# Two attention mixes on one core: the last four tiles of projected rows move from the projection stage into the attention steps

## The chip, the cores and the metric

The kernel runs on one core of a Trainium2 chip. The core has a matrix engine (TensorE, PE in the profile, with its weight loads shown apart as PEld), a vector engine (VectorE, DVE), a scalar engine for activations and copies (ScalarE, ACT), a general engine (GpSimd, POOL) and a queue engine (SyncE, SP) that issues most DMAs. Each engine works through its own instructions in order, and waits on semaphores for the others. The metric is the device time of one execution in microseconds, as the median of several runs.

## The reference

Two attention layers read the same input and are mixed by a gate. Layer A is a full multi-head attention with 32 heads of 18 columns; layer B has 32 query heads but one shared key and value.

```python
def _A_ref(x, wqkv, wo):
    B, S, D = x.shape                       # 1, 2048, 576
    H = 32; Dh = D // H                     # 18
    qkv = (x @ wqkv).reshape(B, S, 3, H, Dh).transpose(2, 0, 3, 1, 4)
    q, k, v = qkv[0], qkv[1], qkv[2]
    scores = jnp.einsum("bhqd,bhkd->bhqk", q, k) * Dh ** -0.5
    p = softmax(scores, axis=-1)
    o = jnp.einsum("bhqk,bhkd->bhqd", p, v)
    return o.transpose(0, 2, 1, 3).reshape(B, S, D) @ wo

def _B_ref(x, wq, wk, wv, wo):
    q = (x @ wq).reshape(B, S, H, Dh).transpose(0, 2, 1, 3)
    k = x @ wk                              # one key and one value for all heads
    v = x @ wv
    scores = jnp.einsum("bhqd,bkd->bhqk", q, k) * (Dh ** -0.5)
    p = softmax(scores, axis=-1)
    o = jnp.einsum("bhqk,bkd->bhqd", p, v)
    return o.transpose(0, 2, 1, 3).reshape(B, S, H * Dh) @ wo

g = sigmoid((x * gate_w).sum(-1, keepdims=True))
return g * a + (1 - g) * b
```

## The kernel before

**Numbers in two parts.** Matmuls run on rounded operands (type float32r). To keep accuracy, an operand is split into a rounded high part ("h") and the rounded remainder ("l"), and a product is taken as hh + lh + hl. `split` makes the parts: a copy that rounds, then a subtraction that rounds. `PROJ` lists the 14 matmuls of one projection (5 chunks of the 576 input columns, the last one holding high and low part in its two halves).

**Heads.** There are 64 heads (`NU`): the 32 of layer B first, then the 32 of layer A. The query and key rows of all heads, with the gate and the shared key and value, are the 1792 output rows of one wide projection. They are cut into 14 tiles (`MT`) of 128 rows by 2048 positions, and a tile into four banks of 512 positions, the size of one PSUM bank.

**Stage one, projection.** The transposed input X stays in SBUF in two parts. `project` forms one bank: 14 matmuls of 512 columns (L156), then `leave` rounds the high part out of PSUM on ScalarE (L162), takes the low part on VectorE (L168), and stores both to the DRAM tensor `qk_d` (POOL's DMA queue). For tiles that hold keys, the difference of the first two key banks goes to `kd_d`. Tiles 0 to 2 are formed while X arrives; tiles 3 to 9 follow as 28 banks in a row. Between banks, SP loads the rows of the first heads back (`bring_row`, one load after each bank and a second after each fourth). In the same stretch the value weights of layer A are loaded, rounded (`split_w`, ScalarE and VectorE) and stored to `wv_d`. The last four tiles, 10 to 13, are formed in 16 further banks, each mixed with six maxima of the first heads; there `leave_lead` evicts on ScalarE and subtracts on Pool, and `store_x` writes X to the DRAM tensor `x_d`. After that X's place in SBUF is given to other tiles.

**Stage two, steps.** 1024 steps follow: head u has steps 16u to 16u+15, one for each block of 128 keys. A step has four scores matmuls (`step_scores`, L530) into a ring of three PSUM banks (`ps`), each read by an exponential on ScalarE (L538); four matmuls for the row maxima of a head 22 steps ahead (`step_max`, L478) into a ring of four banks (`pm`), read by VectorE's maximum (L487); and 16 short matmuls that sum the weighted values (`step_pv`, L544). Scores and maxima use different rows of the array and run in pairs. One pair of key banks in a while is taken together ("x" and "y" in the patterns): ScalarE takes the relu of a difference (L481), and VectorE adds and takes the maximum in one instruction (L484).

**What sets the order.** Each engine's order is written by hand. `emit` walks through a pattern string: "s" a scores matmul with its exponential, "m" a maximum, "x" and "y" the paired one, a digit so many quarters of the sums' matmuls, "U" one unit of other work from the list `todo`. `PLAIN` covers two steps without a unit, `SPARSE` eight steps with one, `DENSE` two steps with one. `SPARSE` is used for 256 steps from step 10 (`VB`), for the value units, and again for 256 steps from step 522, for the first output units; steps 266 to 521 and 778 to 945 are plain. `when(T, f)` calls f at step T. `slow` holds generators with small pieces (normalisation, output weights), of which one piece is issued every other step, mostly on Pool and SP. At steps 10, 26, 42 and so on, `max_rows` turns a head's maxima into two more rows of its queries: VectorE, Pool, then two DMA steps on SP.

**Units.** A value unit (`value_units`) multiplies a block of X, read back from `x_d`, by one half of layer A's value weights, read back from `wv_d`: 14 matmuls of 288 columns (L442) into one `pm` bank, one ScalarE eviction (L444), one store. An output unit (`out_proj`) has 12 matmuls of 288 columns (L692) and one eviction (L695) into the accumulator `oacc`, which takes over the value units' place in SBUF at step 274 (`open_oacc`).

## Time and profile before

| | us |
|---|---|
| median of 3 runs | 2738.43 (2738.14 to 2738.99) |
| the profiled execution's own time | 2739.16 |
| its span | 2737.4 |
| TensorE busy | 2729.2 |
| ScalarE busy | 2443.6 |
| VectorE busy | 2391.7 |
| Pool busy | 271.4 |

How to read it. A group's row gives line, engine, operation, what it writes and reads with shapes, count, busy time and the mean duration of one in ns, and behind a second bar the engine's idle time before such instructions, with what ended it. A row of the timeline gives start, duration, engine, line, operation and count; idle time stands in square brackets. Instructions of one engine overlap: the next one starts before the last one has ended, so the distance of two starts, not the duration, is what an instruction costs its engine. A row of the windows gives the stretch, its length, the busy time of the engines shown with the number of instructions, the granted clock, the DMA engines' busy share and GB/s; with a line given, it counts that line's instructions alone. SPq is the issue of a DMA on the SP queue, not its duration. TensorE is shown as busy nearly all the time because a matmul that waits inside the pipeline counts as busy; whether it waited is seen from the distances of the starts.

### The profile page before, as it was taken

Reading aid. Unit: us, or ns where it says so; the run is one execution under the profiler, and the core shown is the slowest. Engines: PE = TensorE matmul, PEld = TensorE weight load, DVE = VectorE, ACT = ScalarE, POOL = GpSimd, SP = SyncE. Lnnn points to the kernel's source line nnn. Section 1 sums busy time; section 2 is a strip of 40 time slices with the busy share of each in tenths; the row PEclk is TensorE's granted clock in tenths of the full one; section 3 lists DMA queues with packets and bytes.
Section 4 is the critical chain, followed back from the end, with each engine's and each line's share of the span. In section 5 each row is a group of like instructions: output and inputs, shape, how many; then the busy total and the mean of one; then the engine's idle time right before and its main releaser. Section 6 shows DMA issues by size and latency. Waiting matters only on the chain.

```text
span 2737.4 us, 60422 instructions
## 1 busy us (share of the span) xinstructions
PE 2729.2 (100%) x23542; PEld 1301.5 (48%) x23542; DVE 2391.7 (87%) x4495; ACT 2443.6 (89%) x4787; POOL 271.4 (10%) x407
## 2 busy tenths in 40 slices
PE   9999999999999999999999999999999999999999
PEld 8874444454454333333334444444444333334555
DVE  4488888888889999999999898888989999998883
ACT  4338999999999999999999999999999999998776
POOL 2371000010001000100110001000100011011002
PEclk9999999999999999999999999999999999999999
DMA  8883211122111101211133213222321223224312
GB/s 285 326 303 125 60 55 38 59 80 75 42 57 57 56 27 34 65 48 31 47 95 108 87 58 95 93 70 75 100 87 46 68 86 99 67 79 120 101 46 89
DMA packets 145954, 242.09 MB, mean 88 GB/s; under 512 B 53650, under 2 KB 99810, under 8 KB 134092
## 3 DMA queue, kind: packets, MB, share of 16 engines
q1 hardware_dynamic: 131268, 187.13, 22.7%
q0 software_dynamic: 13504, 49.88, 4.8%
q8 instruction: 185, 3.03, 0.5%
q10 hardware_dynamic: 896, 1.23, 0.1%
q14 instruction: 101, 0.83, 0.1%
HBM read 149.61 MB, written 79.78 MB: 84 GB/s over the span
## 4 chain that ended last, share of the span: by engine, by line
PE 99%; DMA 0%; DVE 0%; ACT 0%; issue 0%; ACTq 0%
PE acc L544 38%; PE ps L530 32%; PE pm L478 14%; PE ps L156 6%; PE pm L692 4%; PE pm L442 2%; PE acc L555 1%; PE pm L530 0%; DMA xsh<-xT 0%; PE ps L478 0%; PE ps L692 0%; DVE mx L487 0%; DMA wst<-wall 0%; ACT pt L538 0%; DVE oacc L701 0%; PE pm L739 0%
## 5 line engine op out<-in xcount | busy, mean ns | idle before, releaser
L538 ACT ACTIVATE pt<-ps 128x512 f32<-128x512 f32 x4048 | 2133.8, 612 | 119.9 <-PE pm L478 55.3
L487 DVE TENSOR_REDUCE mx<-pm 128x1 f32<-128x512 f32 x3068 | 1942.5, 684 | 193.9 <-PE pm L478 145.7
L530 PE MATMUL ps<-qs,ksb 56*128 56x512 f32 x2688 | 899.2, 436 | 0.1
L478 PE MATMUL pm<-ksb,qs 54*128 54x512 f32 x2336 | 794.7, 437 | 0.1
L530 PEld LDWEIGHTS ps<-qs,ksb 56*128 56x128 f32 x2688 | 435.0, 184 | 493.8 <-ACT pt L538 465.0
L544 PE MATMUL acc<-pt,vb 128*19 128x256 f32 (+3 forms) x6656 | 579.3, 434 | 0.1
L544 PE MATMUL acc<-pt,vg 128*19 128x256 f32 (+3 forms) x6224 | 553.8, 443 | 0.0
L530 PE MATMUL ps<-qs,ksa 56*128 56x512 f32 x1360 | 454.6, 436 | 0.1
L478 PEld LDWEIGHTS pm<-ksb,qs 54*128 54x128 f32 x2336 | 370.9, 184 | 125.5 <-DVE mx L487 57.6
L478 PE MATMUL pm<-ksa,qs 54*128 54x512 f32 x1232 | 425.9, 439 | 0.0
L484 DVE CUSTOM_DVE_ANT_0 junk<-pm,xb 128x512 bf16<-128x512 f32 x500 | 340.3, 681 | 0.2
L530 PEld LDWEIGHTS ps<-qs,ksa 56*128 56x128 f32 x1360 | 219.4, 184 | 239.4 <-ACT pt L538 221.9
L481 ACT ACTIVATE xb<-pm 128x512 f32<-128x512 f32 x500 | 307.5, 615 | 0.0
L544 PEld LDWEIGHTS acc<-pt,vb 128*19 128x19 f32 x6656 | 125.6, 97 | 216.1 <-issue 192.7
L478 PEld LDWEIGHTS pm<-ksa,qs 54*128 54x128 f32 x1232 | 198.0, 184 | 56.5 <-DVE mx L487 26.0
L544 PEld LDWEIGHTS acc<-pt,vg 128*19 128x19 f32 x6224 | 118.8, 97 | 207.1 <-issue 183.2
L118 POOL CAST mh<-mt 128x32 fp32r<-128x32 f32 x64 | 13.4, 210 | 1719.7 <-DVE mt L495 1719.7
L478 PE MATMUL pm<-kdb,qs 54*128 54x512 f32 x372 | 153.3, 412 | 0.0
L162 ACT ACTIVATE phl<-ps 128x512 fp32r<-128x512 f32 x40 | 23.9, 598 | 71.4 <-PE ps L156 56.8
L156 PE MATMUL ps<-xh,wh 128*128 128x512 f32 (+1 forms) x300 | 85.6, 384 | 0.0
L156 PE MATMUL ps<-xh,wl 128*128 128x512 f32 (+1 forms) x300 | 83.3, 376 | 0.0
L168 DVE TENSOR_TENSOR phl<-ps,phl 128x512 fp32r<-128x512 f32 x40 | 27.7, 692 | 62.7 <-ACT phl L162 46.8
(144 smaller groups left out, 1471.9 us busy)
## 6 DMA issues: line engine op xcount, KB each, us to landing
qs<-qk SPq DMA_DIRECT2D x384, 144.0 KB
qk<-phl POOLq DMA_DIRECT2D x56, 512.0 KB, 5.6
ksa<-qk SPq DMA_DIRECT2D x132, 144.0 KB
ksb<-qk SPq DMA_DIRECT2D x66, 144.0 KB
xv<-x_d SPq DMA_DIRECT2D x16, 576.0 KB
onh<-oh SPq DMA_DIRECT2D x32, 256.0 KB
onl<-ol SPq DMA_DIRECT2D x32, 256.0 KB
oih<-onh SPq DMA_DIRECT2D x16, 512.0 KB
```

The source lines that it names most:

```text
L156: nc.tensor.matmul(fp[:, p0:p0 + g], w[a][:kr, k, :], X[b][:kr, k, x0 + p0:x0 + p0 + g], start=(n == 0), stop=(n == len(PROJ) - 1))
L168: nc.vector.tensor_tensor(hl[:, 1, :], fp, hl[:, 0, :].bitcast(F32), op=OP.subtract)
L442: nc.tensor.matmul(fp[:, 0:288], x[:kr, k if b == "h" else NKT + k, :], w[hf][a][:kr, k, :], start=(n == 0), stop=(n == len(PROJ) - 1))
L478: nc.tensor.matmul(pm, qs[u % 3][b:b + 54, i * P:(i + 1) * P], k, start=True, stop=True)
L481: nc.scalar.activation(MX["x", u, i], pm, AF.Relu)
L484: nc.vector.tensor_tensor_reduce(junk, pm, MX.pop(("x", u, i)), 1.0, -3e38, op0=OP.add, op1=OP.max, accum_out=MX[u][:, i, c:c + 1])
L487: nc.vector.tensor_reduce(MX[u][:, i, c:c + 1], pm, axis=AX.X, op=OP.max)
L530: nc.tensor.matmul(ps, kst(u)[b:b + 56, i * P:(i + 1) * P], qs[u % 3][b:b + 56, c * 512:(c + 1) * 512], start=True, stop=True)
L538: nc.scalar.activation(pt, ps, AF.Exp, scale=SCALE)
L544: nc.tensor.matmul(acc[32 * j:32 * j + 19, a:b], v_of(u, i), PT[u, i, j][:, a:b], start=(i == 0), stop=(i == 15), skip_group_check=True)
L555: nc.tensor.matmul(acc[32 * j:32 * j + 19, 256 * half + a:256 * half + b], v_of(NU - 1, i), pt[:, x + a:x + b], start=(i == 0), stop=(i == ...
L692: nc.tensor.matmul(fp[:, 0:288], x, y, start=(n == 0), stop=(n == len(ops) - 1))
```

## The change

Only tiles 0 to 9 are formed in stage one (`NT = 10`): tiles 3 to 5 as 12 banks in a row, tiles 6 to 9 in the 16 banks that are mixed with maxima. Three row loads follow each of the 12 banks. Tiles 10 to 13, which hold rows of heads 50 to 63, become 32 units of stage two (`row_units`), for which steps 274 to 529 now use `SPARSE`: half a bank each, 14 matmuls of 256 columns with X read back from `x_d` as the moving operand. A row unit evicts on ScalarE, rounds on ScalarE, subtracts on Pool, and stores by SP. Every eighth unit is followed by the next tile's weight split on Pool. The first output units start at step 530 instead of 522, and the accumulator is placed at step 530. The value weights no longer go through `wv_d`: the value units' prologue, at step 2, loads them in four pieces through two staging buffers and splits them on Pool.

```diff
-    wv_d = dram.tile([2, 2, P, NKT * 288], F32, name="wv_d")
...
-    LEAD_T = MT - 4
+    NT = 10
     def tiles_left(WN):
-        for mt in range(3, MT):
+        for mt in range(3, NT):
...
-    for n in range(4 * (LEAD_T - 3)):
-        mt, c, w = next(left)
-        if n in (0, 10):
-            vs = load_wv(n // 10)
-        project(mt, c, w)
-        bring_row()
-        if c == 3:
+    for n in range(4 * (NT - 4 - 3)):
+        project(*next(left))
+        for _ in range(3):
             bring_row()
-        if n in (8, 18):
-            store_wv(n // 10, vs)
...
+    def row_units():
+        pool = L["px"]
+        XR, WR = [], []
...
+        def load_xr(c):
+            XR.append(pool.tile([P, 2 * NKT - 1, 256], F32R, name="xr", bufs=2))
+            dma(XR[-1], x_d[:, :, 256 * c:256 * c + 256])
+        def next_w(mt):
+            W = {y: pool.tile([P, NKT, P], F32R, name=f"wr{y}") for y in "hl"}
+            split(WR.pop(0), W["h"], W["l"], nc.gpsimd, nc.gpsimd)
+            if mt + 1 < MT:
+                load_wr(mt + 1)
+            return W
...
+        for mt in range(NT, MT):
+            for c in range(8):
+                x = XR.pop(0)
+                if (mt, c) != (MT - 1, 7):
+                    load_xr((c + 1) % 8)
+                fp = ps_m.tile([P, 512], F32, name="pm")
+                for n, (a, b, k, kr) in enumerate(PROJ):
+                    nc.tensor.matmul(fp[:, 0:256], w[a][:kr, k, :], x[:kr, k if b == "h" else NKT + k, :],
+                                     start=(n == 0), stop=(n == len(PROJ) - 1))
+                hl = pool.tile([P, 2, 256], F32R, name="rhl", bufs=1)
+                st = pool.tile([P, 256], F32, name="rst", bufs=3)
+                nc.scalar.activation(st, fp[:, 0:256], AF.Copy)
+                nc.scalar.activation(hl[:, 0, :], st, AF.Copy)
+                nc.gpsimd.tensor_tensor(hl[:, 1, :], st, hl[:, 0, :].bitcast(F32), op=OP.subtract)
+                rs = slice(mt * P, (mt + 1) * P)
+                dma(qk_d[:, rs, 256 * c:256 * c + 256].rearrange("a p f -> p a f"), hl)
...
+                if c == 7 and mt + 1 < MT:
+                    w = next_w(mt + 1)
+                yield
...
         for hf in range(2):
-            for i, y in enumerate("hl"):
-                dma(w[hf][y], wv_d[hf, i].rearrange("p (k f) -> p k f", k=NKT))
+            src = wv[:, 288 * hf:288 * hf + 288]
+            main = src[0:512, :].rearrange("(p k) m -> p k m", p=P)
+            for k0, k1 in ((0, 3), (3, 5)):
+                t = L["pool"].tile([P, 16, 76], F32, name="vg", bufs=2)
+                t = t.rearrange("p a b -> p (a b)")[:, 0:288 * (k1 - k0)].rearrange("p (k f) -> p k f", f=288)
+                dma(t[:, 0:min(k1, 4) - k0, :], main[:, k0:min(k1, 4), :])
...
+                split(t, w[hf]["h"][:, k0:k1], w[hf]["l"][:, k0:k1], nc.gpsimd, nc.gpsimd)
...
-    when(VB + 8 * 32 + 8, open_oacc)
-    SEG = ((0, [P] * 4, 450, 518), (4, [P] * 4, 862, 942))
+    RB = VB + 8 * 33
+    when(RB - 8, lambda: (early("px"), todo.append(row_units()), pull(1)))
+    when(RB + 8 * 32, open_oacc)
+    SEG = ((0, [P] * 4, 450, 526), (4, [P] * 4, 862, 942))
...
-        elif any(b <= T < b + 8 * 32 for b in (VB, SEG[0][3] + 4)):
+        elif any(b <= T < b + 8 * 32 for b in (VB, RB, SEG[0][3] + 4)):
             emit(SPARSE, 1)
```

More of the change, by code (lines that the diff above doesn't have):

```diff
@@ L306, in gated_mix_kernel @@
                         WN = prep_w(W.pop(0))
-    vws = ExitStack()
-    vwp = vws.enter_context(tc.tile_pool(name="vwp", bufs=1, side="right"))
-    def load_wv(hf):
-        t = vwp.tile([P, NKT, 288], F32, name="vwst")
-        load5(t, wv[:, 288 * hf:288 * hf + 288])
-        return t
-    def store_wv(hf, st):
-        w = {y: vwp.tile([P, NKT, 288], F32R, name=f"vw{y}") for y in "hl"}
-        split_w(st, w, nc.vector)
-        for i, y in enumerate("hl"):
-            dma(wv_d[hf, i], w[y].rearrange("p k f -> p (k f)"), nc.gpsimd)
     def store_x(i):
@@ L332, in gated_mix_kernel @@
         load_q(u, put=later)
-    LEAD_T = MT - 4
+    NT = 10
     def tiles_left(WN):
-        for mt in range(3, MT):
+        for mt in range(3, NT):
             w = WN
-            if mt + 1 < MT:
+            if mt + 1 < NT:
                 WN = prep_w(W.pop(0))
-            if mt + 3 < MT:
+            if mt + 3 < NT:
                 W.append(load_w(mt + 3))
@@ L346, in gated_mix_kernel @@
     left = tiles_left(WN)
-    for n in range(4 * (LEAD_T - 3)):
-        mt, c, w = next(left)
-        if n in (0, 10):
-            vs = load_wv(n // 10)
-        project(mt, c, w)
-        bring_row()
-        if c == 3:
+    for n in range(4 * (NT - 4 - 3)):
+        project(*next(left))
+        for _ in range(3):
             bring_row()
-        if n in (8, 18):
-            store_wv(n // 10, vs)
     assert not rows_back
-    vws.close()
     small = ctx.enter_context(tc.tile_pool(name="small", bufs=1, side="left"))
@@ L404, in open_ph2 @@
         L["kds"] = [p2.tile([P, 512], F32R, name="kda"), kdb]
-        L["early"] = ExitStack()
-        L["vx"] = L["early"].enter_context(tc.tile_pool(name="vx", bufs=1, side="right"))
+        early("vx")
         for t in L["ks"][:2]:
@@ L410, in open_ph2, with early @@
                 dma(t[b + 54:b + 56, :], ones_r)
+    def early(name):
+        if "early" in L:
+            L["early"].close()
+        L["early"] = ExitStack()
+        L["px"] = L["early"].enter_context(tc.tile_pool(name=name, bufs=1, side="right"))
     def open_oacc():
@@ L415, in open_oacc, with load_wr @@
             .tile([P, 16, D], F32, name="oacc")
+    def row_units():
+        pool = L["px"]
+        XR, WR = [], []
+        def load_wr(mt):
+            WR.append(pool.tile([P, NKT, P], F32, name="wrst"))
+            load5(WR[-1], wall[mt])
+        def load_xr(c):
[7 more added lines that the diff above has]
+            return W
+        load_wr(NT)
+        load_xr(0)
+        w = next_w(NT)
+        yield
[15 more added lines that the diff above has]
+                dma(qk_d[:, rs, 256 * c:256 * c + 256].rearrange("a p f -> p a f"), hl)
+                if c < 2:
+                    KD[mt, c] = st
+                elif c < 4:
+                    cs = slice(256 * (c - 2), 256 * (c - 1))
+                    d = pool.tile([P, 256], F32, name="rd", bufs=1)
+                    nc.gpsimd.tensor_tensor(d, st, KD.pop((mt, c - 2)), op=OP.subtract)
+                    dhl = pool.tile([P, 2, 256], F32R, name="rdhl", bufs=1)
+                    split(d, dhl[:, 0, :], dhl[:, 1, :], nc.gpsimd, nc.gpsimd)
+                    dma(kd_d[rs, 0:2, cs], dhl)
+                    dma(kd_d[rs, 2, cs], dhl[:, 0, :])
+                if c == 7 and mt + 1 < MT:
+                    w = next_w(mt + 1)
+                yield
@@ L417, in value_units @@
     def value_units():
-        pool = L["vx"]
+        pool = L["px"]
         XV = {}
@@ L428, in value_units @@
         for hf in range(2):
-            for i, y in enumerate("hl"):
-                dma(w[hf][y], wv_d[hf, i].rearrange("p (k f) -> p k f", k=NKT))
+            src = wv[:, 288 * hf:288 * hf + 288]
[4 more added lines that the diff above has]
+                dma(t[:, 0:min(k1, 4) - k0, :], main[:, k0:min(k1, 4), :])
+                if k1 == NKT:
+                    for b in (0, 64):
+                        dma(t[b:b + 64, k1 - k0 - 1, :], src[512:576, :])
+                split(t, w[hf]["h"][:, k0:k1], w[hf]["l"][:, k0:k1], nc.gpsimd, nc.gpsimd)
         vst = [pool.tile([P, 16, 19], F32, name=f"vst{i}") for i in range(2)]
@@ L663, in out_proj @@
         nt = len(rows)
-        oacc = L["oacc"]
         fin = t0 == 8
@@ L679, in out_proj @@
         yield
-        w = WO[t0]
+        w, oacc = WO[t0], L["oacc"]
         for q in range(8):
```

## The prediction

> **What bounds the kernel now.** I read the page first (busy shares, then the chain that ended last), and then counted how long each stage takes for one repetition of its pattern.

> ```profile
> span 2737.4 us, 60422 instructions
> PE 2729.2 (100%) x23542; PEld 1301.5 (48%) x23542; DVE 2391.7 (87%) x4495; ACT 2443.6 (89%) x4787; POOL 271.4 (10%) x407
> ...
> PE 99%; DMA 0%; DVE 0%; ACT 0%; issue 0%; ACTq 0%
> PE acc L544 38%; PE ps L530 32%; PE pm L478 14%; PE ps L156 6%; PE pm L692 4%; PE pm L442 2%; PE acc L555 1%; PE pm L530 0%; DMA xsh<-xT 0%; PE ps L478 0%; PE ps L692 0%; DVE mx L487 0%; DMA wst<-wall 0%; ACT pt L538 0%; DVE oacc L701 0%; PE pm L739 0%
> ```

> TensorE carries the whole chain, in every stage. So moving matmuls gains only if they cost less where they go. The windows below run from one repetition of a line to a later one. In order: the projection stage (L162 evicts one bank), the steps with value units (L444 evicts one unit), the steps on the plain pattern (L481 comes once in two steps), the steps with output units (L695). Then all engines over the second and third stretch, and over the first stage.

> ```profile
> 53.40:139.10 85.70, 16.14 (x27) 1.00 0.87 321
> 233.20:856.20 623.00, 12.76 (x31) 1.00 0.19 57
> 884.60:1459.20 574.60, 75.68 (x124) 1.00 0.18 53
> 1470.60:2085.90 615.30, 12.75 (x31) 1.00 0.28 82
> 270.00:860.00 590.00, 590.00 (x5568) 291.48 (x5562) 521.52 (x991) 551.64 (x1087) 20.38 (x44) 1.00 0.19 57
> 885.00:1459.00 574.00, 573.94 (x4958) 218.02 (x4956) 553.47 (x1046) 563.33 (x1116) 45.65 (x69) 1.00 0.18 53
> 45.00:140.00 95.00, 95.00 (x422) 78.49 (x421) 36.30 (x52) 30.77 (x51) 29.48 (x44) 1.00 0.87 318
> ```

> A projected bank takes 85.70/27 = 3.174 us, which is 14 matmuls of 0.227. Eight steps take 623.0/31 = 20.10 us with a value unit, 574.6/31 = 18.54 plain (124 of L481 are 31 times eight steps) and 615.3/31 = 19.85 with an output unit. The granted clock is 1.00 in all of them.

> **The change part by part.**

> *What leaves the first stage.* Tiles 3 to 9 were 28 pure banks; tiles 3 to 5 are 12. The next 16 banks, mixed with first maxima, stay 16 (they are now tiles 6 to 9). So 16 x 3.174 = **50.8 us go**. The value weights' ScalarE and VectorE work and their stores go with it, at no gain: ScalarE is busy 30.77 of 95 us there and TensorE 95 of 95. Three row loads instead of one follow a bank. By their shapes, twelve banks (38 us) write 6.3 MB of rows and 0.8 of key differences, and load 3.7 MB of rows and 1.3 of weights: 12.1 MB, or 318 GB/s, just what this stage moves now without holding TensorE. I cost it at nothing; without that cover it is a rival below.

> *What the units cost TensorE.* 32 units of 14 matmuls of 256 columns join 256 steps that were plain. The next rows are 256-column matmuls at the kernel's start, four to a row (12 from the first row to the last), then a value unit and the scores matmul behind it.

> ```profile
> 15.39 0.64 PE L156 MATMUL ps<-xh,wh 128*128 128x256 f32 x4
> ...
> 16.82 0.28 PE L156 MATMUL ps<-xh,wh 128*128 128x256 f32 x1
> ...
> 411.93 0.79 PE L442 MATMUL pm<-vwh,xv 128*128 128x288 f32 x4
> 412.56 0.69 PE L442 MATMUL pm<-vwl,xv 128*128 128x288 f32 x4
> ...
> 413.75 0.29 PE L442 MATMUL pm<-vwl,xv 128*128 128x288 f32 x1
> 413.97 0.50 PE L530 MATMUL ps<-qs,ksb 56*128 56x512 f32 x1
> ...
> L156 PEld LDWEIGHTS ps<-xh,wh 128*128 128x128 f32 x300 | 53.3, 188 | 14.5 <-ACT pst L185 4.7 <-issue 0.5 <-ACT wh L234 0.2
> ```

> 256 columns take 1.43/12 = 0.119 us, 288 take 1.19/9 = 0.132. That the unit's matmuls set the period is seen from the output units: they have 12 instead of 14, and the period is 0.25 shorter, about 2 x 0.132. So with TensorE alone a row unit's eight steps take 20.10 - 14 x 0.013 = 19.92 us, 1.38 above plain; 32 of them cost 44 us, and the sum would be -6.6. This is the lower bound.

> *What they cost ScalarE.* A value unit has one eviction of 288 columns; a row unit has an eviction of 256 and then a rounding that reads it. The rows: such a pair at 512 (eviction, then rounding; after a second rounding the next instruction), and ScalarE and TensorE around a value unit.

> ```profile
> 142.27 0.60 ACT L185 ACTIVATE pst<-ps 128x512 f32<-128x512 f32 x1 [1.90 <-PE ps L156]
> 142.90 0.63 ACT L187 ACTIVATE phl<-pst 128x512 fp32r<-128x512 f32 x1
> ...
> 155.78 0.63 ACT L187 ACTIVATE phl<-pst 128x512 fp32r<-128x512 f32 x1
> 156.32 0.72 ACT L128 ACTIVATE wh<-wst 128x640 fp32r<-128x640 f32 x1
> ...
> 413.01 0.62 ACT L481 ACTIVATE xb<-pm 128x512 f32<-128x512 f32 x1
> 414.08 0.41 ACT L444 ACTIVATE vst<-pm 128x288 f32<-128x288 f32 x1 [0.45 <-PE pm L442]
> 414.51 1.57 ACT L538 ACTIVATE pt<-ps 128x512 f32<-128x512 f32 x3
> 415.95 0.62 ACT L481 ACTIVATE xb<-pm 128x512 f32<-128x512 f32 x1
> 416.43 3.23 ACT L538 ACTIVATE pt<-ps 128x512 f32<-128x512 f32 x6
> ...
> 414.54 0.39 PE L530 MATMUL ps<-qs,ksb 56*128 56x512 f32 x1
> 414.87 1.05 PE L544 MATMUL acc<-pt,vb 128*19 128x512 f32 x8
> ...
> 417.51 0.73 PE L530 MATMUL ps<-qs,ksb 56*128 56x512 f32 x2
> 418.09 0.49 PE L530 MATMUL ps<-qs,ksb 56*128 56x512 f32 x1
> 418.52 0.85 PE L544 MATMUL acc<-pt,vb 128*19 128x128 f32 x16
> ```

> From 0.60 (512) and 0.41 (288) an eviction of 256 takes 0.39. The rounding starts 0.03 after its end, and the next instruction 0.54 later at 512 columns, some 0.33 at 256. So the first exponential can start 0.75 after the eviction's start, where now it starts 0.43 after: 0.3 us later. Does TensorE feel it? Behind the unit ScalarE runs without a gap: three exponentials, the relu, three more. They start 0.48 apart (three in 414.51 to 415.95) and last some 0.6, so the last of these starts near 417.4 and ends near 418.0, and the scores matmul at 418.09 needs its bank (there are three). The sums' matmuls follow that one after 0.43, where after 414.54 they follow after 0.33: it already waits about 0.1. A delay of 0.3 therefore lands on TensorE there, and it is not won back, since later waits are small. I take 0.28: 19.92 + 0.28 = 20.20 us, 1.66 above plain, x 32 = **53.3 us come**. The upper bound is that all ScalarE time added (0.39 + 0.03 + 0.42 - 0.41 = 0.43) reaches TensorE: 20.35, 58 us, and the sum +7.

> *Value weights.* They are now loaded and rounded at step 2, by Pool.

> ```profile
> 217.93 0.63 POOL L433 MEMSET vst<- 128x304 f32 x2 [5.39 <-PE pm L478]
> ...
> 1313.56 0.66 POOL L118 CAST woh<-wost 128x576 fp32r<-128x576 f32 x1 [2.81 <-DMA wost<-wo]
> ...
> L120 POOL TENSOR_TENSOR wol<-wost,woh 128x576 fp32r<-128x576 f32 x9 | 12.8, 1423 | 0.7
> ...
> 233.30 0.41 ACT L444 ACTIVATE vst<-pm 128x288 f32<-128x288 f32 x1 [1.34 <-PE pm L442]
> ```

> Pool splits 864 and 576 columns for each half (the 576 from the rows, 864 in proportion): 0.99 + 2.13 + 0.66 + 1.42 = 5.2 us, 10.4 for both, and between them the third load waits for a staging buffer (there are two) and takes near 3 us (2.81 is such a wait). Begun at about 222, the first half is ready near 227 (first unit 231), the second near 234. Behind it on Pool stand the memsets of the value staging: they end near 234, and the eviction at 233.30 needs them. ScalarE waits about 0.7 us, once; between 0 and 4.5 if the loads are quick or slow. The rounding of the second head's maxima queues behind them too, but its rows are due six steps (15 us) after. **+0.7 us.**

> *SP and Pool in the row steps.* Each unit puts 1152 KB of x on SP behind the maxima's rows, plus its stores.

> ```profile
> 437.05 0.57 SPq L49 DMA_DIRECT2D xv<-x_d  x1
> ...
> 452.10 0.40 PE L442 MATMUL pm<-vwh,xv 128*128 128x288 f32 x1
> ```

> Issued at such a place it has 15 us until the next unit: at half of the 318 GB/s that the first stage moves it lands in 7.4, at a quarter in 14.8. The row store behind it waits on SP for Pool's subtraction, some 2 us after the unit; what queues behind that are the next head's rows, whose first use is nine steps (22 us) after their issue. I cost both at nothing; a late x would hold TensorE at the unit for as long as it is late. Pool's added work (below 2.5 us a unit, and 2.3 us a tile for weights, by the two Pool rows above) hides in its idle time (20 of 590 us busy). Output units and their accumulator come 8 steps later, at no cost.

> **Sum:** -50.8 + 53.3 + 0.7 = +3.2 us on a profiled execution of 2739.16; the median of the three runs is 2738.43, so 2741.6 us.

> **The rivals.**
> *ScalarE absorbs it* (faster): ScalarE is 93.5% busy in the value stretch and 98% in the plain one, so it has room; if the added time is hidden, -6.6 + 0.7 gives 2732.5. Against it stands the late matmul at 418.09.
> *The delay meets TensorE in full, or twice* (slower): the place is the third scores matmul after a unit. It decides once eight steps take over 20.27 us (50.8 - 0.7 + 5.5 = 55.6, /32 = 1.74 over plain); at 20.35 the time is 2746.
> *The first stage runs into its transfers:* its DMA share is already 0.87. Ten per cent more than 38 us is +4, 2745.
> *Halves cost more than half:* each small matmul still needs a weight load, 188 ns long in the row above. If those set the pace, a unit takes 14 x 0.188 = 2.63 instead of 1.67, and 32 cost 31 us more: 2772. The 0.119 speaks against it, with the same loads. [...]

> **How the numbers follow.** 0.2% of this time is 5.5 us, about what a measurement can tell. Forecast case (2734 to 2744): 0.53. ScalarE absorbs it: 0.17, mostly just beyond the bound. Delay in full: 0.18. Transfers: 0.1. Halves: 0.02. The range 2732.5 to 2747 leaves out the halves, and the ends of the two outer cases. Faster 0.14, same 0.56, slower 0.30.

> **What would show it.** The profile after should have the first stage 51 us shorter; eight steps with row units at 20.2 us (19.9 if absorbed, 20.35 in full); their matmuls 0.12 apart; the scores matmul in the third group behind a unit 0.3 later relative to the unit; one short ScalarE wait at the first value eviction. Longer waits for xr on TensorE, or gaps in the first banks, would make it wrong.

## The result, and the profile after

The changed kernel takes 2749.34 us (2748.64 to 2750.01); the kernel before took 2738.64 in the same comparison. The ratio is 1.0038 (95% interval 1.0028 to 1.0049), so it is slower by 0.4%, or 10.7 us. The forecast was 2741.6 with a range of 2732.5 to 2747: it missed.

The page of the changed kernel, the lines that answer to those of before:

```profile
span 2747.6 us, 62094 instructions
PE 2735.5 (100%) x24278; PEld 1342.7 (49%) x24278; DVE 2367.6 (86%) x4465; ACT 2448.8 (89%) x4821; POOL 309.6 (11%) x451
...
PE 98%; DMA 1%; DVE 1%; POOL 0%; ACT 0%; issue 0%; SPq 0%; DVEq 0%; POOLq 0%; ACTq 0%
```

DMA and VectorE now have 1% of the chain each, where both rounded to nothing before; among the new steps are two loads of value weights and a split of them on Pool. The windows say where the time went. They run from one repetition of a line to a later one: the last pure banks of the first stage are first seen by two rows of the timeline (11 banks apart), then the first interval between two value evictions (L491), the 30 others, the row units (L436), the output units (L741), and all engines over the row stretch.

```profile
53.19 0.60 ACT L161 ACTIVATE phl<-ps 128x512 fp32r<-128x512 f32 x1 [1.95 <-PE ps L155]
88.15 0.60 ACT L161 ACTIVATE phl<-ps 128x512 fp32r<-128x512 f32 x1 [2.57 <-PE ps L155]
...
185.60:208.30 22.70, 0.41 (x1) 0.85 0.26 77
208.30:811.30 603.00, 12.37 (x30) 1.00 0.19 56
850.90:1478.95 628.05, 11.93 (x31) 1.00 0.42 125
1499.10:2114.30 615.20, 12.78 (x31) 1.00 0.27 80
851.00:1479.00 628.00, 627.99 (x5892) 301.41 (x5892) 551.91 (x1047) 587.59 (x1178) 91.34 (x133) 1.00 0.42 125
```

A bank still takes 34.96/11 = 3.178 us, so the denser row loads cost the first stage nothing. Eight steps with a row unit take 628.05/31 = 20.26 us (forecast 20.20), with a value unit 20.10 and with an output unit 19.85, as before. But the first value interval is 22.70 us, and the mean granted clock in it is 0.85. This is that place: SP's load of x at step 2, then Pool, then ScalarE, then TensorE, then all engines in the 8 us behind it.

```profile
167.35 0.59 SPq L49 DMA_DIRECT2D xv<-x_d  x1
...
173.65 0.90 POOL L117 CAST vwh<-vg 128x864 fp32r<-128x864 f32 x1 [11.07 <-DMA vg<-wv]
174.62 2.05 POOL L119 TENSOR_TENSOR vwl<-vg,vwh 128x864 fp32r<-128x864 f32 x1
176.62 0.66 POOL L117 CAST vwh<-vg 128x576 fp32r<-128x576 f32 x1
177.36 1.42 POOL L119 TENSOR_TENSOR vwl<-vg,vwh 128x576 fp32r<-128x576 f32 x1
180.20 0.91 POOL L117 CAST vwh<-vg 128x864 fp32r<-128x864 f32 x1 [1.42 <-DMA vg<-wv]
181.19 2.04 POOL L119 TENSOR_TENSOR vwl<-vg,vwh 128x864 fp32r<-128x864 f32 x1
183.17 0.66 POOL L117 CAST vwh<-vg 128x576 fp32r<-128x576 f32 x1
183.91 1.40 POOL L119 TENSOR_TENSOR vwl<-vg,vwh 128x576 fp32r<-128x576 f32 x1
185.25 0.64 POOL L480 MEMSET vst<- 128x304 f32 x2
...
185.63 0.41 ACT L491 ACTIVATE vst<-pm 128x288 f32<-128x288 f32 x1 [5.00 <-POOL vst L480]
...
181.49 0.29 PE L489 MATMUL pm<-vwl,xv 128*128 128x288 f32 x1
...
186.58 0.50 PE L577 MATMUL ps<-qs,ksb 56*128 56x512 f32 x1 [2.91 <-ACT pt L585]
...
189.71 0.79 PE L577 MATMUL ps<-qs,ksb 56*128 56x512 f32 x1
...
186.50:194.50 8.00, 7.92 (x46) 3.25 (x50) 4.20 (x8) 6.01 (x13) 0.00 (x0) 0.57 0.45 135
```

The unit's last matmul starts at 181.49, so its result can be evicted from about 181.8. ScalarE waits until 185.63, for the memsets that stand behind all of Pool's splits. All exponentials queue behind this eviction in ScalarE's order; three scores banks fill up, and TensorE stops for 2.91 us. Then something comes that the prediction did not have: over the next 8 us the granted clock is 0.57, which is half clock for 2 x 0.43 x 8 = 6.9 us (it is 0.50 from 187.45 to 194.28).

### The profile page after: what moved, and what is told of

The parts are those of the page before. It is cut to its first block, busy times and chain, and to the rows that moved or that the text cites. A ratio compares the mean times of both kernels' runs of the same rounds, so it can differ in the third digit from the quotient of the medians.

```text
span 2747.6 us, 62094 instructions
## 1 busy us (share of the span) xinstructions
PE 2735.5 (100%) x24278; PEld 1342.7 (49%) x24278; DVE 2367.6 (86%) x4465; ACT 2448.8 (89%) x4821; POOL 309.6 (11%) x451
## 4 chain that ended last, share of the span: by engine, by line
PE 98%; DMA 1%; DVE 1%; POOL 0%; ACT 0%; issue 0%; SPq 0%; DVEq 0%; POOLq 0%; ACTq 0%
PE acc L591 37%; PE ps L577 26%; PE pm L525 19%; PE ps L155 5%; PE pm L738 4%; PE pm L489 2%; PE pm L432 2%; PE acc L602 1%; DVE mx L534 0%; PE pm L577 0%; DMA xsh<-xT 0%; DMA vg<-wv 0%; PE ps L525 0%; PE ps L738 0%; POOL vwl L119 0%
## 5 line engine op out<-in xcount | busy, mean ns | idle before, releaser
L591 PE MATMUL acc<-pt,vb 128*19 128x128 f32 (+2 forms) x7136 | 569.2, 416 | 0.0
L591 PE MATMUL acc<-pt,vg 128*19 128x256 f32 (+2 forms) x6256 | 553.1, 442 | 0.0
L591 PEld LDWEIGHTS acc<-pt,vb 128*19 128x19 f32 x7136 | 145.4, 97 | 225.7 <-issue 189.7
L525 PEld LDWEIGHTS pm<-kdb,qs 54*128 54x128 f32 x372 | 68.4, 184 | 0.8
L155 PE MATMUL ps<-xh,wh 128*128 128x512 f32 (+1 forms) x220 | 62.1, 381 | 0.3 <-DVE mx L534 0.3
L155 PE MATMUL ps<-xh,wl 128*128 128x512 f32 (+1 forms) x220 | 59.8, 370 | 0.0
L681 POOL TENSOR_TENSOR ot<-ot,R 128x512 f32<-128x512 f32 x32 | 41.1, 1285 | 145.1 <-DMA R<-r_d 145.1
```

Of the source, the lines that this page charges most:

```text
L155: nc.tensor.matmul(fp[:, p0:p0 + g], w[a][:kr, k, :], X[b][:kr, k, x0 + p0:x0 + p0 + g], start=(n == 0), stop=(n == len(PROJ) - 1))
L525: nc.tensor.matmul(pm, qs[u % 3][b:b + 54, i * P:(i + 1) * P], k, start=True, stop=True)
L591: nc.tensor.matmul(acc[32 * j:32 * j + 19, a:b], v_of(u, i), PT[u, i, j][:, a:b], start=(i == 0), stop=(i == 15), skip_group_check=True)
L681: nc.gpsimd.tensor_tensor(ot[:rows, cs], ot[:rows, cs], R[:rows, cs], op=OP.mult)
```

## The experiments

Theory A: the two parts of the change simply add. The rows save 51 us and cost 32 times what eight steps with a unit take above plain; the value weights cost the late eviction, the pause and the half clock. The rivals put all of it on one part, on the first stage's transfers, or on the step pattern.

**One part alone.** In the first kernel the value weights go the old way; in the second only the value weights' path is changed.

```diff
@@ rows only: the changed kernel with
+            for i, y in enumerate("hl"):
+                dma(w[hf][y], wv_d[hf, i].rearrange("p (k f) -> p k f", k=NKT))
...
+        if n in (0, 5):
+            vs = load_wv(n // 5)
...
+        if n in (4, 10):
+            store_wv(n // 5 - (n == 10), vs)
@@ values only: the kernel before with the value units' new prologue, without load_wv and store_wv
```

> The changed kernel with the value weights prepared as before (rounded by ScalarE and VectorE between the first banks, stored to DRAM, read back). Only the moved rows are left of the change. Theory A (the two parts add; rows cost 32 x 1.72 us and save 51.4, and the value weights at step 2 cost 6.3): about 2743 us, the second value eviction 20.1 us after the first. Rival B (the shortened first stage runs into its transfers: now 12 banks carry the value weights' 3 MB as well): the banks before the mixed ones are stretched and the time is 2746 or more. Rival C (the rows cost all of the change): 2749.

> The kernel before with only the value weights' new path (loaded and rounded by Pool at step 2); the rows stay in the first stage. Theory A: 6.3 us slower than before, 2745, with the same late first eviction, the same TensorE gap near 3 us and a granted clock near 0.57 over the 8 us behind it. Rival C (the late eviction is harmless by itself, the loss is in the rows): 2739 to 2740.

Rows only: 2744.74 us against 2739.26 (ratio 1.0019, 1.0011 to 1.0028), 5.5 slower. Values only: 2744.15 (1.0016, 1.0007 to 1.0025), 4.9 slower. Together 10.4, and the whole change measured 10.7. So the parts add, and neither carries the change by itself. The rows were dearer by 1.7 us than expected; the rival on the transfers (B) is not supported, since the eviction of the first value unit came at 183.25, only 0.5 later than in the memsets-first run below (182.72), where the first stage doesn't carry the value weights; the four kernels with that shorter first stage and the memsets first differ among themselves by 0.8 there (181.94 to 182.72). In the profile of the values alone TensorE pauses 2.1 us and the clock is at half behind it:

```profile
236.43 0.79 PE L520 MATMUL ps<-qs,ksb 56*128 56x512 f32 x1 [2.10 <-ACT pt L528]
...
236.30:243.30 7.00, 6.87 (x40) 3.23 (x42) 3.19 (x6) 5.08 (x11) 0.00 (x0) 0.51 0.43 125
```

**The memsets first.** What was late, the weights or the memsets behind them?

```diff
         w = [{y: pool.tile([P, NKT, 288], F32R, name=f"vw{y}{hf}") for y in "hl"} for hf in range(2)]
+        vst = [pool.tile([P, 16, 19], F32, name=f"vst{i}") for i in range(2)]
+        for t in vst:
+            nc.gpsimd.memset(t, 1.0)
...
-        vst = [pool.tile([P, 16, 19], F32, name=f"vst{i}") for i in range(2)]
-        for t in vst:
-            nc.gpsimd.memset(t, 1.0)
```

> The changed kernel with the two memsets of the value staging placed ahead of Pool's weight splits, nothing else. The first value eviction then needs only the first half of the weights, ready before the first unit. Theory A (the eviction waited for the memsets, not for the weights): the 20.1 us between first and second eviction are back, about 2743. Rival D (the first unit itself waits for weights, or Pool's work disturbs VectorE): no change, 2749.

2744.25 us, 5.0 above the kernel before (1.0017, 1.0008 to 1.0026), where the changed kernel was 10.7 above. The first interval is back, and so is the clock:

```profile
182.70:202.80 20.10, 0.41 (x1) 1.00 0.29 87
```

So the late eviction came from the order on Pool alone. The weights themselves are in time, and loading and splitting them at step 2 has no cost that these runs resolve: 2744.25 us here, 2744.74 with the rows only.

**Where the clock falls.** To price a pause by itself, the kernel before got a number of idle memsets ahead of the first value eviction: 39, 41, 43, 52 and 57.

```diff
-        for t in vst:
+        for t in vst + vst[:1] * 39:
             nc.gpsimd.memset(t, 1.0)
```

> The kernel before with 52 more memsets of 0.315 us on Pool ahead of the first value eviction, no other change: Pool is done near 235.0 us instead of 218.6, so that eviction starts 1.7 us late and TensorE pauses about 0.9 us. Theory F (a pause on TensorE costs its length, and one near 2 us or more also halves the granted clock for 6.83 us): the second eviction comes 20.1 + up to 0.9 after where it would, the granted clock stays 1.00. Rival G (any pause halves the clock): 6.83 us at half clock behind it, 3 to 4 us lost.

> The same with 57 more memsets: Pool is done near 236.5, the eviction is 3.2 us late and TensorE pauses about 2.4 us, between the two pauses seen so far (2.1 and 2.9). Theory F: the granted clock is halved for 6.83 us behind the pause, and the second eviction is about 5 us later than in the kernel before. Rival H (the half clock comes from Pool's split work or its loads, not from the pause): the clock stays at 1.00 and 2.4 us are lost.

> The kernel before with 39 more memsets ahead of the first value eviction. The last two such runs showed that a memset costs 0.404 us in a row, not 0.315, so both were late by 6.6 and 8.4 us, TensorE paused 4.7 and 7.8 us, and the clock was halved for 6.83 and 10.24 us. Now Pool should be done near 234.6, the eviction 1.4 us late and the pause near 0.5. Theory F (a pause below 2 us costs its length alone): granted clock 1.00 throughout, about 0.5 us lost. Rival G (any pause halves the clock): 6.83 us at half clock, 3 to 4 us lost.

> The same with 41: eviction some 2.2 us late, pause near 1.2. Theory F: clock 1.00, about 1.2 us lost. Rival G: half clock for 6.83 us, 4 to 5 us lost.

> The same with 43: eviction some 3.0 us late, pause near 2.1, as in the run with the value weights alone (2.1, half clock for 6.83 us, the second eviction 4.3 us late). Theory F: half clock for 6.83 us, the second eviction 4 to 5 us late.

The rows of TensorE behind the pause, then all engines in the stretch after it, for 39, 41 and 43 memsets:

```profile
235.24 0.50 PE L530 MATMUL ps<-qs,ksb 56*128 56x512 f32 x1 [0.49 <-ACT pt L538]
...
235.20:242.20 7.00, 6.96 (x68) 3.17 (x71) 5.43 (x10) 6.72 (x14) 0.00 (x0) 1.00 0.48 144
```

```profile
236.58 0.50 PE L530 MATMUL ps<-qs,ksb 56*128 56x512 f32 x1 [1.31 <-ACT pt L538]
...
236.50:243.50 7.00, 6.92 (x54) 3.01 (x58) 4.16 (x8) 6.03 (x14) 0.00 (x0) 0.76 0.46 140
```

```profile
237.20 0.49 PE L530 MATMUL ps<-qs,ksb 56*128 56x512 f32 x1 [2.11 <-ACT pt L538]
...
237.20:245.20 8.00, 8.00 (x50) 3.35 (x54) 4.29 (x8) 6.01 (x13) 0.00 (x0) 0.57 0.51 144
```

| TensorE's pause, us | half clock, us | last output unit against the kernel before, us |
|---|---|---|
| 0.49 (39 memsets) | none | +1.0 |
| 1.31 (41) | 3.4 | +3.2 |
| 2.10 (values only) | 6.8 | +4.1 |
| 2.11 (43) | 6.8 | +5.4 |
| 2.91 (the changed kernel) | 6.8 | +5.2, against its twin with the memsets first |
| 4.66 (52) | 6.8 | +7.8 |
| 7.79 (57) | 10.2 | +10.0 |

The half clock's length is twice the missing share of the window: 2 x (1 - 0.76) x 7 = 3.4, 2 x (1 - 0.57) x 8 = 6.9; the trace's own clock records have 3.413, 6.827 and 10.240. The runs with 52 and 57, which were the first of this series, paused longer than meant (4.66 and 7.79 us where about 0.9 and 2.4 were expected), since these memsets stand 0.41 us apart, not 0.315 (last section). Rival H (Pool's splits, not the pause) falls: memsets do the same. Theory F put the limit at 2 us, and that is wrong too: 1.31 us already halve the clock. Rival G, any pause, is too strong: 0.49 does not. What tells the pauses apart is taken up in the last section. The last column is from one execution each, whose start differs by a us or so.

**The unit and its pattern.** Two runs ask what a unit costs against the pattern that it is placed in.

```diff
@@ empty: the kernel before with
-        elif any(b <= T < b + 8 * 32 for b in (VB, SEG[0][3] + 4)):
+        elif any(b <= T < b + 8 * 32 for b in (VB, VB + 8 * 32, SEG[0][3] + 4)):
             emit(SPARSE, 1)
@@ plain with units: the memsets-first kernel with
+        elif RB <= T < RB + 8 * 32:
+            emit(PLAIN * 3 + PLAIN.replace("sm sx 2", "sm U sx 2"), 1)
```

> The kernel before with the wide pattern instead of the plain one in steps 266 to 521, without any unit in it. It measures what a unit costs against its own pattern. Theory A (TensorE's matmuls set the period, so taking a unit of 2.04 us out of a period of 20.10 leaves 18.06, 0.48 less than plain): 32 x 0.48 = 15 us faster, 2723. Rival E (without units both patterns meet the same bound of ScalarE and VectorE near 18.5 us): within 3 us of before.

> The kernel of the memsets-first run, but the 256 steps with row units run on the plain pattern, with one unit in every fourth repetition. Plain takes 18.54 us for eight steps, the empty wide pattern 19.10. Theory A (TensorE sets the period of the plain pattern, so a unit adds its 1.87 us in full): 20.4 us, 32 x 0.15 = 5 us slower than the memsets-first run, 2749. Rival E (plain is held by ScalarE and VectorE and has room for a unit): near 19.5 us, 2720.

The empty wide pattern made the kernel slower: 2758.44 us against 2739.26 (1.0069, 1.0057 to 1.0082), 19.2/32 = 0.60 us more than plain for eight steps, so 19.14. Theory A had 18.06: both theories missed. All engines in its steps 266 to 521:

```profile
885.00:1459.00 574.00, 563.20 (x5272) 248.12 (x5270) 529.73 (x1012) 547.39 (x1079) 45.66 (x69) 1.00 0.16 49
```

TensorE is idle for 10.8 us there, where the plain pattern had 0.1. That is 0.36 of the 0.60 us per eight steps; the rest does not show as idle time, and which wait makes it was not followed up. A unit's matmuls stand in place of waits that the wide pattern has anyway: a value unit of 2.04 us lengthens it by 20.10 - 19.14 = 0.96. In the plain pattern there is no such room:

```profile
861.90:1481.30 619.40, 11.54 (x30) 1.00 0.41 123
```

619.40/30 = 20.65 us, 2.1 above plain and 0.4 above the wide pattern with the same unit. The unit costs what it holds TensorE (1.87) and 0.24 more; A had 20.4. The kernel takes 2767.44 (1.0103, 1.0089 to 1.0117), but only 32 x 0.39 = 12.5 of the 23.2 us above the memsets-first run are the units'. The rest fits a wait that no theory had: at the first output unit TensorE stops 10.08 us for a load, and the clock is at half for 2 x 0.33 x 21 = 13.9 us, a part of them inside the stop. Why that load is late was not followed up.

```profile
1513.33 1.06 PE L738 MATMUL pm<-woh,oih 128*128 128x288 f32 x3 [10.08 <-DMA oih<-onh]
...
1499.00:1520.00 21.00, 10.87 (x63) 5.32 (x61) 5.97 (x12) 7.56 (x16) 0.00 (x0) 0.67 0.62 184
```

By the windows, then, the wide pattern is the better one with units and the worse one without them.

**ScalarE's second instruction.** The remaining dispute is the 0.28 us that I let pass from ScalarE to TensorE. One run takes the rounding off ScalarE, one doubles it, both on the memsets-first kernel.

```diff
-                nc.scalar.activation(hl[:, 0, :], st, AF.Copy)
+                nc.gpsimd.tensor_copy(hl[:, 0, :], st)
@@ and, in the other kernel
                 nc.scalar.activation(hl[:, 0, :], st, AF.Copy)
+                nc.scalar.activation(hl[:, 0, :], st, AF.Copy)
```

> The kernel of the memsets-first run with one more edit: the high part of a row unit is rounded by Pool instead of ScalarE, so ScalarE has one eviction of 256 columns in a unit and no second instruction that waits for it. Theory A (the second ScalarE instruction pushes the exponentials back by 0.3 us and the third scores matmul behind the unit passes it on): eight steps with a row unit go from 20.26 to 19.95 us, 10 us less in all, 2734, below the kernel before. Rival E (the empty wide pattern already takes 19.10, so the period is set by the pattern's own waits and the unit only fills them; the rounding is hidden): 20.2, 2743.

> The kernel of the memsets-first run with the ScalarE rounding of a row unit issued twice (the second repeats the first). Taking the rounding off ScalarE brought eight steps from 20.26 to 19.93 us. Theory A (ScalarE time behind the unit passes one to one to TensorE, from the third scores matmul on): one more rounding, some 0.3 to 0.4 us, gives 20.6 us and 2755. Rival I (the first 0.3 were a step that is now taken, a wait for one bank, and further ScalarE time is hidden): 20.3, 2745.

The row units' windows (31 intervals each) with the memsets first, with the rounding on Pool, and with two roundings on ScalarE:

```profile
845.75:1473.90 628.15, 11.89 (x31) 1.00 0.42 125
```

```profile
844.65:1462.30 617.65, 11.96 (x31) 1.00 0.43 127
```

```profile
845.10:1486.70 641.60, 11.89 (x31) 1.00 0.41 122
```

20.26, 19.92 and 20.70 us: 0.34 less and 0.43 more. The kernel with two roundings takes 2757.67 us (1.0069, 1.0046 to 1.0092). 19.92 is what the prediction worked out for TensorE alone. The first exponential starts 0.37, 0.79 and 1.24 us after the unit's eviction without, with one and with two roundings on ScalarE. So of the 0.42 us that the first rounding adds there, 0.34 reach the period, and of the second's 0.45 all but 0.02. ScalarE time behind the unit passes on nearly in full, and the rivals that hide it fall. With the rounding on Pool the kernel takes 2733.98 us against 2739.13 (0.9981, 0.9972 to 0.9990): of all kernels run it is the fastest, 5.2 us below the kernel before.

## Why the prediction was wrong

*First stage.* Predicted -50.8. The first value eviction came at 233.30 before and at 182.72 with the memsets first: -50.6. Right to within the scatter of starts (0.8 us), and the transfers cost nothing that can be seen.

*Units, TensorE.* 0.119 us a matmul: in the changed kernel the last nine distances of a row unit take 1.08 us, 0.12 each (1031.80 to 1032.88). 19.92 us for eight steps: confirmed by the run without the rounding. That halves cost more than half did not happen. The reading behind it was too simple, though: TensorE's matmuls add to the period in this pattern, but an emptied pattern does not give their time back (19.14, not 18.06).

*Units, ScalarE.* The mechanism was right, the size a little small. ScalarE behind a row unit, then TensorE, in the changed kernel:

```profile
1033.20 0.39 ACT L436 ACTIVATE rst<-pm 128x256 f32<-128x256 f32 x1 [0.28 <-PE pm L432]
1033.66 0.42 ACT L437 ACTIVATE rhl<-rst 128x256 fp32r<-128x256 f32 x1
1033.99 1.56 ACT L585 ACTIVATE pt<-ps 128x512 f32<-128x512 f32 x3
...
1033.09 0.50 PE L577 MATMUL ps<-qs,ksb 56*128 56x512 f32 x1
...
1036.80 0.50 PE L577 MATMUL ps<-qs,ksb 56*128 56x512 f32 x1
1037.13 0.91 PE L577 MATMUL ps<-qs,ksb 56*128 56x512 f32 x2
1037.55 0.49 PE L525 MATMUL pm<-kdb,qs 54*128 54x512 f32 x1
```

The first exponential starts 0.79 after the eviction (predicted 0.75). The maximum that runs beside the third group's third scores matmul starts 4.46 after the first one of the unit's followers (1037.55 - 1033.09); before it was 418.09 - 413.97 = 4.12. That is 0.34 later where I took 0.28, and x 32 the term is 55.2 instead of 53.3.

*Value weights: the step that failed.* The prediction said that the memsets "end near 234, and the eviction at 233.30 needs them. ScalarE waits about 0.7 us, once", +0.7. The wait was named and placed rightly, and Pool's part took what was said: the splits 0.9, 2.05, 0.7 and 1.4 us, and from the first split to the memsets 11.6 us (173.65 to 185.25) where the prediction has 12 (222 to 234). Three things were wrong. First, the start: the splits began 8.1 us before the unit's result (173.65 to 181.8), where the prediction has 11.2 (222 to 233.2). Of these 3.1 us, 2.0 are the first load (6.3 us from the x load's issue to the first split, 167.35 to 173.65, where I gave 4.3, 217.7 to "about 222"); the other 1.1 are SP, which issued the x load that much later relative to the unit. These are the rows of before, the x load and the unit's last matmul (those of after stand above):

```profile
217.68 0.60 SPq L49 DMA_DIRECT2D xv<-x_d  x1
...
232.91 0.30 PE L442 MATMUL pm<-vwl,xv 128*128 128x288 f32 x1
```

So the eviction was 3.8 us late instead of 0.7. Second, the price: I passed ScalarE's wait to the sum as it was, without asking what TensorE does meanwhile. Every exponential stands behind the eviction and TensorE has three banks, so about 0.9 us of the wait are covered and the other 2.91 are a pause; with 39 memsets, too, a wait 1.3 us longer than before gave a pause of 0.49. By these two, as an estimate, a wait of 0.7 would have cost nothing. Third, I had no term at all for the half clock behind a pause. Pause and half clock together are 5.5 us: the second value eviction came at 208.32, against 202.84 with the memsets first. My own bound for late loads, 4.5, was not carried into the range together with that for ScalarE either: -50.8 + 58 + 4.5 = +11.7 would have put the upper end at 2750.

The sum as measured: -50.6 + 55.2 + 5.5 = +10.1 us; the two profiled executions differ by 2749.38 - 2739.16 = 10.2. That they agree to 0.1 is luck, since the start of the value units alone scatters by 0.8. Of the miss of 7 to 8 us, some 4.8 belong to the value weights and 1.9 to the rounding.

*SP and Pool in the row steps.* No TensorE time was lost to late x; Pool was busy 91 of 628 us. Right.

## What to carry to other kernels

When work is put in front of an instruction on a quiet engine, look at what else stands behind it on that engine, and at who is next in line: two memsets of 0.3 us each, moved ahead of the splits, were worth 5 us here. On a path where TensorE is the bound, ask of a pause of about 1.3 us or more whether the half clock follows; in the table above, pause and half of the stretch at half clock together are about the most that was lost. And where an eviction and a rounding follow each other on a busy engine right behind a unit, count both, with their dependence, against the next bank that TensorE needs; give the second one to an engine that has time.

## What the runs showed of the hardware

A pause of TensorE of 0.49 us left its clock alone (1.00 over the 7 us behind it); pauses of 1.31 to 7.79 us in the steps came with 3.413, 6.827 or 10.240 us at half clock, one, two or three times the same length, and the 10.08 us of the plain pattern with units with 13.653, four times. With 52 and 57 memsets the half clock began inside the pause, since behind it only 2 x 0.35 x 7 = 4.9 and 2 x 0.37 x 7 = 5.2 us are left:

```profile
240.80:247.80 7.00, 6.98 (x54) 3.28 (x58) 4.07 (x8) 5.89 (x12) 0.00 (x0) 0.65 0.48 142
```

```profile
242.60:249.60 7.00, 6.98 (x50) 3.30 (x54) 3.92 (x8) 5.74 (x12) 0.00 (x0) 0.63 0.46 139
```

What goes with the fall here is TensorE's idle time inside one stretch of this length, not the pause's length as such. Of some 11,000 such stretches at full clock in the fourteen traces, laid end to end from that start and short of the one that holds the kernel's last matmul, the seven with 1.31 us or more of idle time, as the profile counts it, were followed by the half clock, and none with 1.26 or less was. The closest pair, first from the run with 52 memsets (a pause in its first stage, and the stretch that holds it), then from the run with 41 (the stretch that holds its pause, and the next one):

```profile
203.76 0.47 PE L530 MATMUL ps<-qs,ksb 56*128 56x512 f32 x1 [1.26 <-issue]
201.31:204.72 3.41, 2.15 (x13) 1.27 (x11) 1.48 (x3) 1.68 (x3) 3.24 (x4) 1.00 0.98 369
204.72:208.13 3.41, 3.41 (x17) 2.54 (x16) 2.06 (x4) 0.63 (x2) 3.07 (x4) 1.00 0.42 163
...
235.02:238.44 3.42, 2.11 (x18) 0.80 (x14) 1.45 (x5) 2.81 (x7) 0.92 (x4) 1.00 0.05 12
238.44:241.85 3.41, 3.41 (x30) 1.35 (x22) 1.90 (x4) 2.98 (x7) 0.00 (x0) 0.50 0.42 114
```

Idle time alone does not decide it, though. The stretch that holds the last matmul has 1.75 us of it in the kernel before and 1.38 in the changed kernel, and the next one, all idle, is still at 1.00. The rows of before, then those of after:

```profile
2730.86:2734.27 3.41, 1.66 (x13) 1.43 (x11) 2.05 (x5) 0.41 (x1) 1.36 (x2) 1.00 0.99 366
2734.27:2737.35 3.08, 0.00 (x0) 0.00 (x0) 0.00 (x0) 0.00 (x0) 0.00 (x0) 1.00 0.56 210
```

```profile
2740.61:2744.03 3.42, 2.04 (x16) 1.81 (x14) 2.19 (x6) 0.46 (x2) 1.61 (x2) 1.00 0.99 369
2744.03:2747.44 3.41, 0.00 (x0) 0.00 (x0) 0.00 (x0) 0.00 (x0) 0.00 (x0) 1.00 0.61 228
```

Whether a pause that two stretches share may be longer without loss was not shown; of such, the traces have one of 0.97 us (rows only, at 1065.06), which lost no clock. What decides how many lengths at half clock follow stays open, and so does a limit: the two stretches of the closest pair hold different work (projection and steps).

With 52 idle memsets ahead of the first value eviction, Pool's memsets (128 x 304) that write the same tile one after the other stand 0.41 us apart, those that change the tile 0.29. There are 54. The first three write the first tile, the second and the first again; all others write the first. The rows of the first three and of all 54, then the group's row:

```profile
218.01 0.93 POOL L433 MEMSET vst<- 128x304 f32 x3 [5.29 <-PE acc L544]
...
218.01 21.82 POOL L433 MEMSET vst<- 128x304 f32 x54 [5.29 <-PE acc L544]
...
L433 POOL MEMSET vst<- 128x304 f32 x54 | 18.9, 352 | 8.2 <-PE acc L544 5.3
```

Each takes 0.35 us. The first three start (0.93 - 0.35)/2 = 0.29 us apart and so overlap; the others (21.82 - 0.93)/51 = 0.41 apart, with Pool idle for 0.06 between two of them. Why was not shown: no run here changes the tile alone.
